# A chain of attention and two expert layers on one core: another order for the product of two weight matrices, three staging slots, and a last contraction made in halves

## The chip, the core and the metric

The kernel runs on one core of a Trainium2 chip. The metric is device microseconds (us) of one execution, from its begin to its end. Five engines of the core are spoken of: PE (TensorE, the matmuls), DVE (VectorE), ACT (ScalarE), POOL (GpSimd) and SP (SyncE, which here only issues transfers). Each works through its own instructions strictly in order. Results of matmuls stand in eight PSUM banks, `bk0` to `bk7`; a bank can be written again when what it holds has been read. TensorE's clock has two levels, 1.2 and 2.4 GHz; the profile gives the mean that was granted in a stretch, as a share of the higher one.

## The reference, cut to what matters

```python
def _attn_ref(q, k, v):                      # batch 4, heads 8, seq 576, head_dim 64
    scores = (1.0 / np.sqrt(D)) * np.matmul(q, k.transpose(0, 1, 3, 2))
    mask_plain = (rel >= 0) & (rel < 32)                       # heads 0 to 3
    mask_dil = (rel >= 0) & (rel < 128) & (rel % 4 == 0)       # heads 4 to 7
    attn = softmax(np.where(mask, scores, -1e9))
    return np.matmul(attn, v)

def _moe_ref(x, w1, w2, w3, w_out):          # d_model 512, d_ff 1024
    h = (x @ w1) * (x @ w2) @ w3
    return h @ w_out

def _moe2_ref(x, w_gate, w_val, w_out):      # d_model 512, d_ff 1536
    g = x @ w_gate
    return (g / (1.0 + np.exp(-g)) * (x @ w_val)) @ w_out

def reference(...):
    x = attention output as (4 * 576, 8 * 64)                  # 2304 tokens x 512
    return _moe2_ref(_moe_ref(x, ...), ...)
```

The weights arrive as float64; q, k and v are float32.

## The kernel before

**Precision.** Each operand of a large matmul is held as a high and a low part (`to_parts`: ACT copies the high part, L163, and DVE subtracts it from the source for the low one, L164). One product is then three matmuls, high by high, high by low and low by high (`mm3`, L221 to L223). The float64 weights are turned into float32 by `to_float32`, one ACT instruction (L204) and two on DVE (L205, L206), and split (ACT L199, DVE L200).

**Stage 0, from the start to about 94 us: attention of the first batch and W = w3 @ w_out.** Since nothing stands between `w3` and `w_out`, their product W (1024 x 512) is made once. It is eight tiles of 128 rows, each a sum over eight blocks j of three matmuls 128x512, 192 matmuls. The weights come in blocks of 1 MB, two names each, in the order of the list `W_ORDER`, through five buffers (`raw0` to `raw2` and two parts of `early`) that are loaded again as soon as they are converted. A program of sixteen steps s (L469) gives the order: in the first eight the tiles 0 to 3 are summed on `bk4`, `bk5`, `bk0` and `bk1` (names `w3a`), in the last eight the tiles 4 to 7 on `bk2`, `bk3`, `bk0` and `bk1` (names `w3b`). Between the steps stand units of attention, of head pairs 0 to 3 of the first batch: for each pair two halves of scores (L326; DVE scale and mask L340, maximum L343, ACT exp L345, DVE L348 to L350), three transposes (L363, ACT copy `pt` L365) and two halves of values (L378), whose results `to_parts` writes into `x0`, the input of the first expert layer. The units take their PSUM banks from `att_banks` in turn, which is `bk6`, `bk7` and, until the fourth block has been converted, also `bk2` and `bk3` (L314, L468).

**Stage 1, about 87 to 430 us: the first expert layer by chunks of tokens.** Chunks 0 to 3 have 512 tokens, chunk 4 has 256. For each of eight k: `gate_a` (12 matmuls, then ACT L240 copies the bank to `ta`), `gate_b` (12 matmuls, then DVE L246 multiplies, and `to_parts` makes `p`) and the contraction with W of the k before (12 matmuls). Attention of the following batch is interleaved in chunks 0 to 2. The weights of the second layer are staged beside it (`quarters`): a block is converted, DVE makes four sums of quarters (L535 to L538), and seven operands are split, the high part by ACT (L517) and the low one by POOL (L518), into a stage tile of 896 KB, which SP stores to `wd` or `wod` in DRAM (L554). A block gives two stage tiles. There are two stage tiles that take turns; a copy L517 into one waits until the store of what it held has landed. In chunks 3 and 4 the two lie in `mid_u` (L600).

**Stage 2, about 425 us to the end: the second expert layer.** Three parts of 768 tokens, six steps each, by seven products instead of eight: for each step the products of `w_gate` and `w_val` (L704, 128x384), whose results are put together by ACT and DVE (L710 to L724) into `u`, and for every two steps a contraction with the third matrix (`units`, L749): its seven operands are made by `make` (DVE sums L627 and `to_parts`) into four slots `po0` to `po3`, and its matmuls (L782) go into `bk0` to `bk3`, from where DVE adds them to `acc` (L768). The contraction of q, the q-th such pair of nine, runs between the products of the pair after it. The last, q = 8, has none after it and runs alone at the end, before the result is stored (L771).

The order in which each engine takes its instructions is fixed ahead of the run by a scheduler, within what program order, tiles and banks allow. PE's order is the same in both kernels from the middle of chunk 0 to chunk 4.

## Time and profile before

| | us |
|---|---|
| three runs | 856.11, 857.17, 857.97 |
| median | 857.17 |
| the profiled execution | 856.14 |
| its span, first to last instruction | 854.4 |
| outside the span | 1.74 |

| engine | busy us | share of the span |
|---|---|---|
| PE | 827.0 | 97% |
| DVE | 527.4 | 62% |
| ACT | 427.0 | 50% |
| POOL | 131.6 | 15% |

The mean granted clock was 0.992. PE is busy in 97% of the span, so a reader looks for the stretches where it is not. Where the profile names a releaser of an idle stretch, it is the work whose end came last among those that the instruction waited for. Because matmuls are pipelined, the distance between the starts of two of them is what one costs in a row, and it is less than the duration shown.

### The profile page before, as it was taken

The numbers are of one execution on the slowest core, as the hardware profiler recorded it, in microseconds if no ns is written. First come the engines' busy times: TensorE is split into PE (matmuls) and PEld (weight loads), VectorE is DVE, ScalarE is ACT, GpSimd is POOL, SyncE is SP. The second block draws the span as 40 slices with busy tenths as digits, with TensorE's granted clock in tenths as the row PEclk, the third lists the DMA queues.
The fourth block names the chain that finished last, engine by engine and source line by source line (L and its number), as shares of the span: only waits on it lengthen the run. The fifth ranks groups of instructions, "written<-read, shape, count | busy, mean of one in ns | idle before, by whom it ended". The sixth has DMA issues, their size and how long they took to land.

```text
span 854.4 us, 13410 instructions
## 1 busy us (share of the span) xinstructions
PE 827.0 (97%) x4954; PEld 751.8 (88%) x4954; DVE 527.4 (62%) x890; ACT 427.0 (50%) x1002; POOL 131.6 (15%) x180
## 2 busy tenths in 40 slices
PE   7879999999999899999899999999999999999996
PEld 5668888888888788877799999999999999999996
DVE  5899966275526652444566646588645677554747
ACT  4697765465635554334455544354444454353422
POOL 1000144135502541064520000000000000000000
PEclk8999999999999999999999999999999999999999
DMA  9997557568655845666999877788978787977725
GB/s 283 342 318 258 173 159 251 160 194 300 174 176 180 263 149 163 203 208 202 317 323 362 312 249 256 244 297 274 323 260 259 238 269 239 319 260 250 243 77 169
DMA packets 93248, 207.09 MB, mean 242 GB/s; under 512 B 7424, under 2 KB 56704, under 8 KB 88448
## 3 DMA queue, kind: packets, MB, share of 16 engines
q1 hardware_dynamic: 90304, 201.53, 72.2%
q10 hardware_dynamic: 2880, 4.72, 1.6%
q8 instruction: 39, 0.64, 0.3%
q14 instruction: 25, 0.20, 0.1%
HBM read 162.45 MB, written 43.78 MB: 241 GB/s over the span
## 4 chain that ended last, share of the span: by engine, by line
PE 76%; DMA 12%; DVE 6%; ACT 3%; POOL 2%; issue 1%; SPq 1%; ACTq 0%; DVEq 0%; POOLq 0%
PE bk L221 23%; PE bk L222 23%; PE bk L223 23%; DMA raw<-w_in 4%; DMA early<-w_in 3%; PE bk L326 3%; POOL u L518 2%; DMA wd<-u 2%; PE bk L378 2%; DMA wod<-u 2%; PE bk L363 1%; DMA k<-k_in 1%; DVE raw L206 1%; DVE w L200 1%; ACT s L345 1%
## 5 line engine op out<-in xcount | busy, mean ns | idle before, releaser
L221 PE MATMUL bk<-x,w 128*128 128x512 f32 (+2 forms) x400 | 146.6, 367 | 3.9 <-ACT ta L240 3.9
L223 PE MATMUL bk<-x,w 128*128 128x512 f32 (+2 forms) x400 | 146.4, 366 | 0.0
L222 PE MATMUL bk<-x,w 128*128 128x512 f32 (+2 forms) x400 | 146.0, 365 | 0.1
L221 PE MATMUL bk<-w 128*128 128x384 f32 (+1 forms) x264 | 93.2, 359 | 0.2 <-ACT w L199 0.2
L222 PE MATMUL bk<-w 128*128 128x384 f32 (+1 forms) x264 | 92.5, 352 | 0.5 <-DVE w L200 0.5
L221 PEld LDWEIGHTS bk<-x,w 128*128 128x128 f32 x400 | 75.4, 188 | 16.1 <-ACT ta L240 6.7
L223 PE MATMUL bk<-w 128*128 128x384 f32 (+1 forms) x264 | 89.4, 350 | 0.0
L222 PE MATMUL bk<-po,wo 128*128 128x384 f32 x252 | 84.4, 336 | 1.4 <-DVE po L164 1.4
L221 PE MATMUL bk<-po,wo 128*128 128x384 f32 x252 | 83.5, 336 | 1.7 <-ACT po L163 1.7
L223 PE MATMUL bk<-po,wo 128*128 128x384 f32 x252 | 84.6, 336 | 0.0
L768 DVE TENSOR_TENSOR acc<-bk,acc 128x384 f32<-128x384 f32 x102 | 55.8, 553 | 46.2 <-PE bk L223 46.0
L222 PEld LDWEIGHTS bk<-x,w 128*128 128x128 f32 x400 | 75.4, 189 | 10.1 <-DVE x L164 0.5
L223 PEld LDWEIGHTS bk<-x,w 128*128 128x128 f32 x400 | 75.4, 189 | 9.6
L518 POOL TENSOR_TENSOR stage<-raw,stage 128x256 fp32r<-128x256 f32 x88 | 63.9, 754 | 59.0 <-ACT stage L517 59.0
L163 ACT ACTIVATE po<-u 128x768 fp32r<-128x768 f32 x63 | 52.5, 843 | 31.3 <-PE bk L223 15.3
L710 ACT ACTIVATE u<-bk 128x384 f32<-128x384 f32 x80 | 38.8, 490 | 56.7 <-PE bk L223 55.6
L164 DVE TENSOR_TENSOR po<-u,po 128x768 fp32r<-128x768 f32 x63 | 59.6, 952 | 8.9 <-ACT po L163 8.8
L204 ACT ACTIVATE raw<-raw 128x1024 f32<-128x1024 f32 (+1 forms) x33 | 37.4, 1133 | 49.7 <-DMA raw<-w_in 49.7
L246 DVE TENSOR_TENSOR ta<-bk,ta 128x512 f32<-128x512 f32 (+1 forms) x40 | 25.4, 634 | 57.3 <-PE bk L223 28.4
L222 PE MATMUL bk<-p,W 128*128 128x512 f32 (+1 forms) x160 | 58.9, 373 | 0.2 <-DVE p L164 0.2
L223 PE MATMUL bk<-p,W 128*128 128x512 f32 (+1 forms) x160 | 58.9, 372 | 0.0
L221 PE MATMUL bk<-p,W 128*128 128x512 f32 (+1 forms) x160 | 57.1, 376 | 1.8 <-ACT p L163 1.8
(114 smaller groups left out, 1748.7 us busy)
## 6 DMA issues: line engine op xcount, KB each, us to landing
w<-wd SPq DMA_DIRECT2D x70, 512.0 KB, 4.6
wo<-wod SPq DMA_DIRECT2D x63, 512.0 KB, 4.7
raw<-w_in SPq DMA_DIRECT2D x31, 1024.0 KB, 9.0
mid<-wd SPq DMA_DIRECT2D x42, 512.0 KB, 4.6
wd<-stage SPq DMA_DIRECT2D x16, 896.0 KB, 6.3
wd<-u SPq DMA_DIRECT2D x8, 896.0 KB, 5.0
x<-wd SPq DMA_DIRECT2D x14, 512.0 KB, 4.5
v<-v_in SPq DMA_DIRECT2D x16, 432.0 KB, 8.2
```

The lines of the kernel that those rows point to most:

```text
L163: nc.scalar.activation(hi, src, AF.Copy)
L164: return nc.vector.tensor_tensor(out=lo, in0=src, in1=hi.bitcast(F32), op=ALU.subtract)
L204: nc.scalar.activation(hi.bitcast(F32), hi.bitcast(F32), AF.Prelu, scale=REBIAS, alpha=SIGN_UP)
L221: nc.tensor.matmul(ps, wh, xh, start=start, stop=False, skip_group_check=onto)
L222: nc.tensor.matmul(ps, wh, xl, start=False, stop=False, skip_group_check=onto)
L223: nc.tensor.matmul(ps, wl, xh, start=False, stop=stop, skip_group_check=onto)
L246: nc.vector.tensor_tensor(out=u, in0=bb[:, :n], in1=ta[:, :n], op=ALU.mult)
L326: nc.tensor.matmul(ps[:, (n - b0) * KW:(n - b0 + 1) * KW], q[:, QB + 2 * QB * n:QB + 2 * QB * (n + 1)], kk[:, n * QB:n * QB + KW], start=T ...
L378: nc.tensor.matmul(ps[j * D:(j + 1) * D, lo - a:hi - a], v_of(i)[:KW, n, j * D:(j + 1) * D], pt[:KW, n, (j + n) % 2 * QB + lo - n * QB:(j ...
L518: nc.gpsimd.tensor_tensor(out=dst[:, :, 1], in0=src, in1=dst[:, :, 0].bitcast(F32), op=ALU.subtract)
L710: nc.scalar.activation(t, src, AF.Copy)
L768: nc.vector.tensor_tensor(out=a, in0=ps, in1=a, op=ALU.add)
```

## The change

It has three parts.

*The product W and attention before chunk 0.* The same twelve blocks of weights, each as large as before, come in another order, and the columns of `w3` are cut into three pieces: `w3a` (tiles 0 to 3, as before), `w3c` (tiles 4 and 5) and `w3d` (tiles 6 and 7). The tiles 4 and 5 are summed on `bk2` and `bk3` while tiles 0 to 3 are summed on their four banks; then tile 6 is made over all j on `bk2`, and tile 7 on `bk3`. `att_banks` is `bk6` and `bk7` from the start. The matmuls that the blocks converted so far allow are 12, 24, 24, 48, 48, 72, 72, 96, 120, 144, 168, 192 before, and 12, 24, 36, 48, 72, 72, 96, 108, 120, 144, 168, 192 after.

*Staging in chunks 3 and 4.* There are three stage tiles instead of two, in `mid_u` from column block 1 on, and the low parts are subtracted by DVE instead of POOL: 56 instructions, 42 of 128x256 and 14 of 128x128. In chunks 0 to 2 two stage tiles and POOL remain.

*The last contraction.* The operands of q = 8 are made in two halves of 128x384, one for each step j of its pair: the first halves during the last products (`half(0)`), the second ones after (`half(1)`). Two of every six operands go to slots in `w_all` (`spare_ops`), the others to `po0` to `po3`.

```diff
-for _j in range(2, K1, 2):
-    W_ORDER += [(("wo1", _j), ("wo1", _j + 1)), (("w3a", _j), ("w3a", _j + 1))]
-W_ORDER += [(("w3b", j), ("w3b", j + 1)) for j in range(0, K1, 2)]
+for _name, _j in ("w3c", 0), ("wo1", 2), ("w3a", 2), ("wo1", 4), ("w3a", 4), ("w3c", 2), ("wo1", 6), ("w3a", 6), ("w3d", 0), ("w3d", 2):
+    W_ORDER.append(((_name, _j), (_name, _j + 1)))
...
+W_NEEDS = [1, 2, 3, 4, 5, 5, 7, 7, 8, 9, 10, 10, 11, 11, 12, 12]
...
-            att_banks = batt + acc[2:]
+            att_banks = batt
...
-            for upto in (2, 9, 16):
-                next_block()
-                attend(upto)
             next_block()
-            del att_banks[2:]
-            for s in range(2 * K1):
...
+            attend(2)
+            def w_step(name, i):
+                w3 = slot_of[name, i]
+                if name == "w3a":
+                    js, tiles, banks = [i], range(4), [ba, bb, acc[0], acc[1]]
+                elif name == "w3c":
+                    js, tiles, banks = [2 * i, 2 * i + 1], range(4, 6), acc[2:]
+                else:
+                    js, tiles, banks = range(i % 2 * 4, i % 2 * 4 + 4), [6 + i // 2], [acc[2 + i // 2]]
...
+            for s, step in enumerate(W_STEPS):
+                while n_split[0] < min(W_NEEDS[s] + 1, N_W1) and free:
                     next_block()
...
+                w_step(*step)
+                attend(min(4 * s + 5, done_at[1]))
...
             def split_to(dst, src):
                 nc.scalar.activation(dst[:, :, 0], src, AF.Copy)
-                nc.gpsimd.tensor_tensor(out=dst[:, :, 1], in0=src, in1=dst[:, :, 0].bitcast(F32), op=ALU.subtract)
+                (nc.gpsimd if len(stages) == 2 else nc.vector).tensor_tensor(out=dst[:, :, 1], in0=src, in1=dst[:, :, 0].bitcast(F32), op=ALU.subtract)
...
-                    stage = stages[n_stage[0] % 2]
+                    stage = stages[n_stage[0] % len(stages)]
...
-            stages[:] = [mid_u.rearrange("p n t -> p (n t)")[:, 8 * HT + i * 1792:8 * HT + (i + 1) * 1792].bitcast(F32R) for i in range(2)]
+            stages[:] = [mid_u.rearrange("p n t -> p (n t)")[:, HT + i * 1792:HT + (i + 1) * 1792].bitcast(F32R) for i in range(3)]
...
+            def made_at(q, r):
+                if q == NQ - 1:
+                    return spare_ops[r % 6] if r % 6 < 2 else late[0][(NPROD * q + r - 2) % NPO]
+                return late[0][(NPROD * q + r) % NPO]
...
+            def half(j):
+                if not halves[j]:
+                    u = uq[(NQ - 1) % 2]
+                    halves[j] = list(enumerate(sums([[u[:, 0, j], u[:, 1, j]], [u[:, 2, j], u[:, 3, j]]], C_ORDER)))[::-1]
+                r, of = halves[j].pop()
+                o = made_at(NQ - 1, r)
+                to_parts(of(), o[:, 0, j], o[:, 1, j])
...
                             if m == 1:
                                 load_wo(t + NWO)
+                                if q == NQ - 2 and 3 <= r < 6 or q == NQ - 1 and r == 0:
+                                    half(0)
+                                if q == NQ - 1 and r < NPROD - AHEAD1:
+                                    half(1)
...
+                        if n == FP * NC2 - 1:
+                            if m == 0 and i < 2:
+                                half(0)
+                            if m and i in (S3, S4):
+                                half(1)
```

What stands on three engines at three places follows. Lines of the changed kernel lie further down by 4 at the first place (L164, L200, L205, L206, L398 and L340 become L168, L204, L209, L210, L402 and L344), by 4 and 12 at the second (L163 and L240 become L167 and L244, L517 becomes L529), and by up to 29 at the third (L627, L722 and L768 become L639, L734 and L797). `raw0`, `raw1`, `raw2` and `early` are buffers of arriving weights, `w` is the memory of converted ones, `W2` and `W3` are tiles 4 to 7 of W, and `bk` is a bank.

DVE, at the end of stage 0, up to the last piece of `x0` (head pair 3), before:

```order
L206 SCALAR_TENSOR_TENSOR raw2_108<-raw2_108 128x1024
L200 TENSOR_TENSOR w_66<-raw1_79,w_66 128x2x512
L164 TENSOR_TENSOR W2_74<-bk2_84,W2_74 128x512
L164 TENSOR_TENSOR W2_74<-bk3_85,W2_74 128x512
L205 TENSOR_SCALAR raw0_78<-raw0_78 128x1024
L200 TENSOR_TENSOR w_66<-raw2_108,w_66 128x2x512
L164 TENSOR_TENSOR W3_75<-bk0_82,W3_75 128x512
L206 SCALAR_TENSOR_TENSOR raw0_78<-raw0_78 128x1024
L164 TENSOR_TENSOR W3_75<-bk1_83,W3_75 128x512
L164 TENSOR_TENSOR x0_76<-bk6_88,x0_76 128x2x128
```

The same place after:

```order
L168 TENSOR_TENSOR W3_75<-bk3_85,W3_75 128x512
L210 SCALAR_TENSOR_TENSOR raw2_108<-raw2_108 128x1024
L204 TENSOR_TENSOR w_66<-raw1_79,w_66 128x2x512
L209 TENSOR_SCALAR raw0_78<-raw0_78 128x1024
L204 TENSOR_TENSOR w_66<-raw2_108,w_66 128x2x512
L210 SCALAR_TENSOR_TENSOR raw0_78<-raw0_78 128x1024
L168 TENSOR_TENSOR x0_76<-bk7_89,x0_76 128x2x128
L402 COPY o0_80<-bk7_89 128x2x16
L168 TENSOR_TENSOR x0_76<-bk6_88,x0_76 128x2x128
```

The tiles of W have moved ahead of the conversions; the conversions themselves, of the same blocks of w1 and w2, still stand ahead of the last piece of `x0`.

ACT, in chunk 3, at the second staged block (`raw0`; `u` is the stage tile, `ta` the first gate, `p` the operand of the contraction), before:

```order
L240 ACTIVATE ta_68<-bk4_86 128x512
L517 ACTIVATE u_2876<-raw1_79 128x2x128 x4
L163 ACTIVATE p_77<-ta_68 128x512
L517 ACTIVATE u_2876<-raw0_78 128x2x128
L517 ACTIVATE u_2876<-raw0_78 128x128
L240 ACTIVATE ta_68<-bk4_86 128x512
L517 ACTIVATE u_2876<-raw0_78 128x2x128 x5
```

The same place after:

```order
L244 ACTIVATE ta_68<-bk4_86 128x512
L529 ACTIVATE u_2876<-raw1_79 128x2x128 x4
L167 ACTIVATE p_77<-ta_68 128x512
L244 ACTIVATE ta_68<-bk4_86 128x512
L529 ACTIVATE u_2876<-raw0_78 128x2x128
L529 ACTIVATE u_2876<-raw0_78 128x128
```

The copy to `ta` has moved ahead of the first copies of the second block into a stage tile.

DVE, after the last product's results (`g`), in the last contraction (`po` and, after, `w` are its operands), before:

```order
L768 TENSOR_TENSOR acc_3803<-bk0_82,acc_3803 128x384
L722 TENSOR_TENSOR u_2876<-bk5_87,g_2874 128x384
L627 TENSOR_TENSOR u_2876<-u_2876 128x768
L164 TENSOR_TENSOR po1_3796<-u_2876,po1_3796 128x768
L768 TENSOR_TENSOR acc_3803<-bk2_84,acc_3803 128x384
L164 TENSOR_TENSOR po3_3798<-u_2876,po3_3798 128x768
L627 TENSOR_TENSOR u_2876<-u_2876 128x768
L164 TENSOR_TENSOR po0_3795<-u_2876,po0_3795 128x768
```

The same place after:

```order
L168 TENSOR_TENSOR po1_3796<-u_2876,po1_3796 128x384
L734 TENSOR_TENSOR u_2876<-bk5_87,g_2874 128x384
L168 TENSOR_TENSOR po2_3797<-u_2876,po2_3797 128x384
L797 TENSOR_TENSOR acc_3803<-bk2_84,acc_3803 128x384
L797 TENSOR_TENSOR acc_3803<-bk1_83,acc_3803 128x384
L168 TENSOR_TENSOR w_66<-u_2876,w_66 128x384
L797 TENSOR_TENSOR acc_3803<-bk3_85,acc_3803 128x384
L168 TENSOR_TENSOR po0_3795<-u_2876,po0_3795 128x384
```

Behind the last multiplication (L722, now L734) operands of 128x768 with their sums have given way to halves of 128x384; their first halves stand ahead of it.

## Rows read from the trace of the kernel before

**Rows 1.** Windows: length; PE, PEld, DVE, ACT, POOL busy (count); clock; DMA; GB/s

```profile
9.28:53.46 44.18, 35.81 (x233) 28.98 (x233) 36.59 (x67) 31.61 (x90) 0.00 (x0) 0.89 1.05 338
40.33:93.82 53.49, 49.04 (x322) 39.76 (x320) 51.74 (x78) 42.72 (x83) 0.00 (x0) 0.97 0.84 283
50.00:60.00 10.00, 7.13 (x30) 6.05 (x31) 10.00 (x17) 8.91 (x20) 0.00 (x0) 0.83 0.98 274
365.00:430.00 65.00, 59.03 (x300) 49.04 (x299) 32.83 (x51) 26.98 (x64) 33.19 (x45) 1.00 0.77 252
829.60:836.48 6.88, 5.44 (x32) 5.12 (x31) 6.88 (x12) 2.89 (x4) 0.00 (x0) 1.00 0.35 88
```

**Rows 2.** Timeline of PE, stage 0: start, duration, line, operation [idle before <-releaser]

```profile
53.46 2.02 PE L326 MATMUL bk<-k,q 128*128 128x96 f32 x8
...
86.70 0.39 PE L223 MATMUL bk<-w 128*128 128x512 f32 x1
86.93 0.39 PE L221 MATMUL bk<-x,w 128*128 128x512 f32 x1
...
93.87 0.50 PE L222 MATMUL bk<-x,w 128*128 128x512 f32 x1
```

**Rows 3.** Timeline of DVE, stage 0

```profile
40.33 0.70 DVE L205 TENSOR_SCALAR raw<-raw 128x1024 uint32<-128x1024 uint32 x1 [2.78 <-DMA raw<-w_in]
40.94 1.12 DVE L340 SCALAR_TENSOR_TENSOR s<-bk,mask 128x480 f32<-128x480 f32 x2
...
93.21 0.60 DVE L164 TENSOR_TENSOR x<-bk,x 128x256 fp32r<-128x256 f32 x1
```

**Rows 4.** Waits of PE by releaser, 365 to 430 us: total us, times, longest

```profile
PE bk L221 <- ACT ta L240: 3.9, 5, 1.1
...
PE bk L221 <- ACT p L163: 1.8, 1, 1.8
```

**Rows 5.** Timeline of all engines, chunks 3 and 4

```profile
363.89 4.90 POOL L518 TENSOR_TENSOR u<-raw,u 128x256 fp32r<-128x256 f32 x6
...
365.71 1.31 DVE L164 TENSOR_TENSOR p<-ta,p 128x512 fp32r<-128x512 f32 x1 [1.14 <-ACT p L163]
...
369.91 0.43 DVE L535 TENSOR_TENSOR raw<-raw 128x256 f32<-128x256 f32 x1
...
374.22 0.63 ACT L517 ACTIVATE u<-raw 128x256 fp32r<-128x256 f32 x2 [8.54 <-DMA wod<-u]
...
375.39 0.50 PE L221 MATMUL bk<-x,w 128*128 128x512 f32 x1 [0.80 <-ACT ta L240]
...
377.86 0.69 DVE L164 TENSOR_TENSOR p<-ta,p 128x512 fp32r<-128x512 f32 x1 [1.80 <-ACT p L163]
...
426.38 1.17 ACT L204 ACTIVATE raw<-raw 128x1024 f32<-128x1024 f32 x1 [1.76 <-DMA raw<-w_in]
```

**Rows 6.** Transfers issued in 365 to 430 us: KB each, median us to landing

```profile
wd<-u SPq DMA_DIRECT2D x8, 896.0 KB, 5.0
raw<-w_in SPq DMA_DIRECT2D x5, 1024.0 KB, 9.2
wod<-u SPq DMA_DIRECT2D x4, 896.0 KB, 6.8
```

**Rows 7.** Timeline of PE at the end

```profile
832.97 0.33 PE L221 MATMUL bk<-w 128*128 128x384 f32 x1
...
833.49 0.33 PE L221 MATMUL bk<-po,wo 128*128 128x384 f32 x1
...
836.48 0.44 PE L222 MATMUL bk<-po,wo 128*128 128x384 f32 x1 [1.44 <-DVE po L164]
...
840.17 0.79 PE L221 MATMUL bk<-po,wo 128*128 128x384 f32 x3 [1.67 <-ACT po L163]
...
850.70 0.34 PE L223 MATMUL bk<-po,wo 128*128 128x384 f32 x1
```

**Rows 8.** Timeline of DVE at the end

```profile
835.47 0.95 DVE L164 TENSOR_TENSOR po<-u,po 128x768 fp32r<-128x768 f32 x1
```

More of the change, by code (lines that the diff above doesn't have):

```diff
@@ L83 @@
 NPO = 4
+AHEAD1 = 4
 NWO = 4
@@ L104, in moe_chain_kernel @@
         fp = first_pool.__enter__()
-        wslot = [w_all[:, i] for i in (6, 1, 3, 0, 5, 2, 7, 4)] + [fp.tile([P, 2, 2, 512], F32R, name=f"W{i}") for i in range(4)]
+        wslot = [w_all[:, i] for i in (2, 3, 7, 4, 0, 6, 1, 5)] + [fp.tile([P, 2, 2, 512], F32R, name=f"W{i}") for i in range(4)]
         xb = [fp.tile([P, 2, KT, CMAX], F32R, name="x0")]
@@ L463, in moe_chain_kernel @@
             free.extend(wslot[:8])
-            for upto in (2, 9, 16):
-                next_block()
-                attend(upto)
             next_block()
-            del att_banks[2:]
-            for s in range(2 * K1):
-                h, j = divmod(s, K1)
-                while n_split[0] < min(s // 2 * 2 + 4, N_W1) and free:
-                    next_block()
-                wo, w3 = slot_of["wo1", j], slot_of["w3b" if h else "w3a", j]
-                banks = [acc[2], acc[3], acc[0], acc[1]] if h else [ba, bb, acc[0], acc[1]]
-                for kk in range(4):
-                    c = slice(kk * P, (kk + 1) * P)
-                    mm3(banks[kk], (w3[:, 0, c], w3[:, 1, c]), (wo[:, 0], wo[:, 1]), j == 0, j == K1 - 1)
-                if j == K1 - 1:
-                    for kk in (2, 3, 0, 1):
-                        w = wslot[8 + 2 * h + kk // 2][:, kk % 2]
-                        slot_of["W", 4 * h + kk] = w
-                        to_parts(banks[kk], w[:, 0], w[:, 1])
-                release(("w3b" if h else "w3a", j))
-                if h:
-                    release(("wo1", j))
-                attend(min(4 * s + 4, done_at[1]))
+            attend(2)
@@ new lines, in w_step @@
+            def w_step(name, i):
[6 more added lines that the diff above has]
+                    js, tiles, banks = range(i % 2 * 4, i % 2 * 4 + 4), [6 + i // 2], [acc[2 + i // 2]]
+                n = 0
+                for j in js:
+                    wo = slot_of["wo1", j]
+                    for ps in banks:
+                        c = slice(n * P, (n + 1) * P)
+                        mm3(ps, (w3[:, 0, c], w3[:, 1, c]), (wo[:, 0], wo[:, 1]), j == 0, j == K1 - 1)
+                        n += 1
+                if js[-1] == K1 - 1:
+                    for kk, ps in zip(tiles, banks):
+                        w = wslot[8 + kk // 2][:, kk % 2]
+                        slot_of["W", kk] = w
+                        to_parts(ps, w[:, 0], w[:, 1])
+                release((name, i))
+                if name == "w3d" and i >= 2:
+                    release(*[("wo1", j) for j in js])
@@ L747, in load_wo @@
                     nc.sync.dma_start(out=dst.bitcast(F32), in_=src.bitcast(F32))
+            def made_at(q, r):
+                if q == NQ - 1:
+                    return spare_ops[r % 6] if r % 6 < 2 else late[0][(NPROD * q + r - 2) % NPO]
+                return late[0][(NPROD * q + r) % NPO]
+            NQ = FP // 2 * NC2
+            spare_ops = [ops[i] for i in range(NOP) if (i - NPROD * (NC2 - 1)) % NOP >= NPROD]
+            halves = [[], []]
+            def half(j):
[5 more added lines that the diff above has]
+                to_parts(of(), o[:, 0, j], o[:, 1, j])
             def units(q):
                 u = uq[q % 2]
-                made = deque(enumerate(sums([[u[:, 0], u[:, 1]], [u[:, 2], u[:, 3]]], C_ORDER)))
+                made = deque(enumerate(sums([[u[:, 0], u[:, 1]], [u[:, 2], u[:, 3]]], C_ORDER)) if q < NQ - 1 else [])
                 c, first = divmod(q, FP // 2)
@@ L758, in make @@
                         r, of = made.popleft()
-                        o = late[0][(NPROD * q + r) % NPO]
+                        o = made_at(q, r)
                         to_parts(of(), o[:, 0], o[:, 1])
@@ L778, in unit @@
                             t = NPROD * q + r
-                            w, x = late[1][t % NWO], late[0][t % NPO]
+                            w, x = late[1][t % NWO], made_at(q, r)
                             ps = cbank[m][s in (S1, S4, A12)][:, :HT]
@@ L816, in moe_chain_kernel @@
                             step()
+                        if n == FP * NC2 - 1:
[3 more added lines that the diff above has]
+                                half(1)
                 if n % 2:
                     units(n // 2)
+            half(0)
+            for _ in range(AHEAD1 - 2):
+                half(1)
             contract_some(99)
@@ L864, in layouts @@
         "w3a": lambda j: rows(w3t, j)[:, :512],
-        "w3b": lambda j: rows(w3t, j)[:, 512:],
+        "w3c": lambda j: np.concatenate([rows(w3t, 2 * j + i)[:, 4 * P:6 * P] for i in range(2)], 1),
+        "w3d": lambda j: np.concatenate([rows(w3t, j % 2 * 4 + i)[:, (6 + j // 2) * P:(7 + j // 2) * P] for i in range(4)], 1),
         "w1": lambda j: cols(w1, j),
```

2 lines of the change are left out of this document (added).

## The prediction, made before the change was run

> **What bounds the kernel now.** PE is busy in 97% of the span, so I looked for the stretches in which it is not, first in the windows, then in each stretch with the waits and the timelines. Three stretches matter, and each has another limit.
>
> *Stage 0.* In 9.28 to 53.46 us PE is busy for 35.81 of 44.18 us [rows 1], 8.4 us idle, at a granted clock of 0.89. From 53 us on it runs through: the last matmul of the product W starts at 86.70, the first of chunk 0 at 86.93 [rows 2]. But DVE tells more. From 40.33 us, where it has waited 2.78 us for weights, to 93.82 us, when the last piece of `x0` is done (L164 at 93.21, 0.60 long) [rows 3], it is busy for 51.74 of 53.49 us [rows 1]. PE needs that piece for its matmul at 93.87 [rows 2]. So DVE, not the product, sets when chunk 0 can go on. PE's idle time before was not lost; it only let PE come out at the time at which DVE was ready.
>
> *Staging in chunks 3 and 4.* In 365 to 430 us PE is busy for 59.03 of 65.00 us [rows 1], 5.97 idle: 3.9 waiting for ACT's copy to `ta` in five stalls, 1.8 for its copy to `p` in one [rows 4], and short rests. ACT is busy for only 26.98 us there. The chain is seen at 374.22: the first copy L517 into a stage tile has waited 8.54 us for the store `wod<-u` of what the tile held; the copy to `ta` stands behind it, and PE goes on at 375.39, 0.80 late [rows 5].
>
> *The end.* The last product's matmuls end ahead of 833.49. Then PE runs the last contraction and stops at 836.48 for 1.44 us (DVE's `po`) and at 840.17 for 1.67 us (ACT's `po`); its last matmul starts at 850.70 [rows 7]. DVE has no pause in 829.60 to 836.48 [rows 1].
>
> **Part 1, the product W.** The 192 matmuls, the twelve blocks, their bytes and their conversions remain. What PE can start earlier it starts earlier: 36 matmuls instead of 24 after the third block. The 8.4 us of idle time could so go, and the product end at about 78.5 instead of 86.9. What comes next is the last piece of `x0`. From the L205 that waits at 40.33 up to that piece DVE has the same instructions in both orders, conversions of the blocks 6 to 17 and half of block 18, eight pieces of W, six of `x0`, four softmax halves, but for two that have moved ahead of 40.33 and so into the 2.78 us of waiting: a mask (half of 1.12 for two [rows 3]) and a maximum of the same size, 1.1 us together. If DVE has no pauses, the piece is done at 40.33 + 51.7 - 1.1 = 91.0; with all its pauses of before, at 93.8 - 1.1 = 92.7. I take the middle, 91.9: 2.0 us gained. Against it stands the clock. PE will now stand idle for much of the ten microseconds between the end of the product and this piece, as it did in 50 to 60 us, where the granted clock was 0.83 with PE busy for 7.13 of 10 us [rows 1]. A mean of 0.83 is a third of the time at 1.2 GHz; it costs up to 0.17 x 10 = 1.7 us if the matmuls behind it run in it, nothing if none does; I take 1.1, nearer to the full price, since matmuls follow at once. Net 0.9 us gained. Bounds: 2.8 gained (no pause, no clock lost) and 1.5 lost (the pauses of before leave 1.2 of gain, the full clock price takes 1.7, and 1.0, another pause of DVE like those that it has now in sum, if two banks instead of four hold up a softmax).
>
> The Trainium skill (Perfetto Trace Analysis, Identifying Performance Opportunities) says that the same gap coming again and again on the engine that should be saturated can mean too few SBUF or PSUM buffers for the next tile. That speaks against taking two of attention's four banks away; if the trace followed it, the loss would be that of the rival on pair 3 below. The trace of before can't settle it: it shows the scores on four banks, and none that waits long for one.
>
> **Part 2, staging.** 5.97 us of idle time, and each of the six stalls is followed by a matmul 0.50 instead of 0.39 long [rows 2, 5], 0.7 in all: 6.7 us to be had. A block gives two tiles at once. With two slots, the first tile of a block waits for the first of the block before, whose store takes 5.0 to 6.8 us to land at the median [rows 6]; with three, each tile has at least one block more time, and a k of 36 matmuls at 0.227 (86.70 to 86.93 [rows 2]) is 8.2 us long. In chunk 3 this takes the wait away: ACT's copy to `ta` has also moved ahead of the second block's copies. In chunk 4 a k is about half as long, a block needs 9.2 us to land [rows 6], ACT waited 1.76 us for one at 426.38 [rows 5], and a third slot does nothing for that. I keep 2.0 us of stalls there, between 0 and 4. So 4.7 gained, from 2.7 to 6.7.
>
> The subtraction moves from POOL (4.90 for six [rows 5], 0.82 each) to DVE, where 128x256 takes 0.43 [rows 5]: 56 x 0.43 = 24 us at the most. DVE is busy for 32.83 of 65 us there [rows 1], 57 at the most after. Some of that comes back: L164 took 1.31 us at 365.71, within POOL's 4.90 from 363.89, and 0.69 at 377.86 [rows 5], and POOL now rests. What it adds is a wait: DVE's subtraction now stands in order behind ACT's copy, and if that copy waits for a slot, DVE's L246 and L164 wait behind it. They need ACT's `ta` and `p` anyway, which stand behind the same copy, so I cost it at nothing; without that cover each wait would be worth a stall like those of before, about 1 us, and the lower end above holds two of them.
>
> **Part 3, the end.** Behind the last product 78 matmuls remain before, 72 after (six move ahead of it). From 832.97 to 833.49 are three steps, 0.173 each [rows 7], so without a stall the last would start at 833.49 + 77 x 0.173 = 846.8 rather than at 850.70: 3.9 us of stalls, 3.1 in the two large ones. The six that move change nothing in the sum. Afterwards the first halves of the operands are made before the last product ends, and what follows DVE's last multiplication is a half each, instead of operands of 128x768 at 0.95 us [rows 8] with their sums. Halving costs more per element (0.43 for 256 columns against 0.69 for 512 [rows 5]), some 14 extra instructions in all, which DVE has room for after 836.48, not before. I see no operand that comes late by more than a few tenths, and keep 0.6 us for reads of banks. So 3.3 gained; at worst 1.5 (one of the two stalls stays), at best 3.9. The store after it, 3.4 us from the last matmul to the end, stays.
>
> **Sum.** 0.9 + 4.7 + 3.3 = 8.9 us off the profiled 856.14: 847.2. That execution lies 1.03 below the median of 857.17, so 848.3 for the median. The ends of the terms give 13.4 (843.8) and 2.7 (854.5).
>
> **The rivals.**
> *DVE is not the limit of stage 0.* If earlier tiles of W let DVE skip ahead and the piece of `x0` comes as early as the product, all 8.4 us come back: 848.3 - 7.5 = 840.8. Against it: 51.7 us of DVE work that is still there.
> *Transfers limit the staging, and stage 0 gives nothing.* The DMA share is 0.77 in 365 to 430 us and 0.84 in stage 0 [rows 1]; a faster ACT asks for blocks earlier and waits for their 9.2 us. Then staging gives half, 2.5, stage 0 nothing: 857.17 - 2.5 - 3.0 = 851.7.
> *Nothing is gained, for the change doesn't do what it says.* The stalls of staging turn into waits for blocks, PE's clock eats what stage 0 brings, and the end still waits for one operand: 857 or a little under.
> *Slower: attention on two banks delays pair 3.* The second half of its scores runs on PE at 53.46 now [rows 2]; 40.4 us later PE has its `x0`. With two banks each unit waits until ACT or DVE has read the one before the last. I estimate the scores at 60 from the units ahead of them, which is still ahead of DVE's queue. If they come after 63, the chain of softmax, transposes and values, if it remained as long as now, would bring the piece after 103; that is 9.5 us more than 93.9, less than the rest gains by 1.5. At 65 the piece would come at 105, 11 us late: 857.2 + 11 - 8.0 = 860.
>
> **How the numbers follow.** The forecast has 0.62, the early `x0` 0.06, the transfers 0.17, no gain 0.08, slower 0.07. About two in ten lie outside 843.8 to 854.5, to which the forecast and the transfers belong with nearly all of theirs. This kernel can be told from no change by about 0.2%, 1.7 us: faster 0.85, same 0.08, slower 0.07.
>
> **What would show it.** In the profile after: the last piece of `x0` between 91 and 92.7 us, PE idle before it for several us, at a lower clock; no L221 wait for `ta` over 0.3 us in chunk 3, some in chunk 4; no POOL row in chunks 3 and 4; the last matmul within 13.5 us of the last product. Wrong would be: a piece of `x0` much earlier or later, waits of DVE for ACT's copies into stage tiles with PE behind, or a stall of over 1 us in the last contraction.

## The result, and the profile after

The changed kernel takes 847.77 us at the median (six runs, 845.88 to 852.09), the kernel before, run beside it, 859.31. Their ratio, taken over all these runs, is 0.9883, 95% interval 0.9848 to 0.9918 (the two medians alone would give 0.9866). Its profiled execution took 847.58 us, span 845.6; the forecast for that sum was 847.2, and 848.3 for the median. In two later jobs the ratio was 0.9901 (0.9871 to 0.9931) and 0.9917 (0.9886 to 0.9947).

Page of the changed kernel, part 1, and its windows, of which the third, fourth and sixth answer to [rows 1]. Columns as there. Lines of the changed kernel lie 4 to 29 further down, as said with the change.

```profile
PE 825.4 (98%) x4954; PEld 751.7 (89%) x4954; DVE 539.6 (64%) x957; ACT 429.4 (51%) x1009; POOL 89.2 (11%) x124
...
9.28:53.46 44.18, 39.25 (x236) 32.19 (x237) 37.85 (x62) 31.99 (x82) 0.00 (x0) 0.92 1.05 335
40.33:93.82 53.49, 47.85 (x322) 38.47 (x321) 52.43 (x79) 45.58 (x86) 0.00 (x0) 0.95 0.86 289
...
80.00:90.00 10.00, 5.48 (x61) 4.06 (x60) 10.00 (x14) 6.84 (x10) 0.00 (x0) 0.95 0.50 158
90.00:95.00 5.00, 4.89 (x16) 3.87 (x17) 4.82 (x10) 2.84 (x3) 0.00 (x0) 0.50 0.40 154
95.00:100.00 5.00, 5.00 (x31) 4.44 (x30) 4.53 (x11) 3.94 (x15) 0.00 (x0) 0.92 0.44 117
365.00:430.00 65.00, 63.28 (x348) 54.99 (x347) 47.48 (x109) 31.60 (x75) 0.00 (x0) 1.00 0.87 287
```

The kernel before, the same windows at the end of stage 0:

```profile
80.00:90.00 10.00, 10.00 (x79) 7.98 (x78) 9.69 (x14) 9.17 (x13) 0.00 (x0) 1.00 0.61 211
90.00:95.00 5.00, 4.88 (x28) 3.89 (x26) 5.00 (x9) 1.97 (x4) 0.00 (x0) 1.00 0.44 177
```

PE is idle for 1.7 of the 65 us from 365 to 430, where it had been idle for 5.97. In 80 to 90 it is idle for 4.5 us, where it had run through, and the clock granted right behind is 0.50, the lower of its two levels, where it had been 1.00.

To see where the time went, the start of the same matmul was read in the traces of before and of the other kernel at five places: the first of the contraction with W in chunk 1, in chunk 3 at k = 2 (the 313th of these matmuls), the first of the second layer's contraction, the first of its last pair (q = 8), and the very last. The differences between neighbouring places, in us (minus is earlier than before):

| kernel | to chunk 1 | chunks 1, 2 | chunks 3, 4 | stage 2 | end | sum |
|---|---|---|---|---|---|---|
| changed, first | +0.16 | -0.38 | -5.24 | 0.00 | -3.27 | -8.73 |
| changed, again | -0.22 | +1.05 | -5.18 | 0.00 | -3.28 | -7.63 |
| changed, third | -0.72 | +4.88 | -2.97 | 0.00 | -3.27 | -2.08 |
| a_old_product | -0.64 | +1.75 | -4.44 | 0.00 | -3.30 | -6.63 |
| product_only | -0.19 | +2.86 | -1.45 | 0.00 | -0.16 | +1.06 |
| b_three_pool | -0.42 | +0.62 | +0.03 | 0.00 | -3.27 | -3.04 |
| c_two_dve | -0.47 | -0.87 | +3.84 | -1.04 | -3.26 | -1.80 |
| d_old_tail | -0.46 | +2.57 | -5.10 | 0.00 | -0.11 | -3.10 |
| e_warm | -4.65 | +13.33 | -2.54 | 0.00 | -3.30 | +2.84 |
| f_pool_w | +2.77 | +1.64 | -4.67 | 0.00 | -3.28 | -3.54 |
| g_warm8 | +0.76 | +4.97 | -5.64 | 0.00 | -3.26 | -3.17 |
| h16 | -4.74 | +9.46 | -2.53 | 0.00 | -3.27 | -1.08 |
| h15 | -6.91 | +6.19 | -4.68 | 0.00 | -3.27 | -8.67 |

The first row is the answer for that execution: nothing from the product W, 5.2 from staging, 3.3 from the end. How far one execution can be trusted is told by the columns in which kernels are alike. In chunks 1 and 2, where PE's order is the same in both kernels, three executions of the changed kernel differ by 5 us. Windows from the mark of chunk 1 to that of chunk 3, of the first and of the third:

```profile
188.90:371.49 182.59, 180.61 (x1128) 148.84 (x1126) 94.49 (x186) 93.71 (x283) 56.81 (x77) 1.00 0.62 200
188.02:375.87 187.85, 184.38 (x1127) 151.06 (x1126) 95.09 (x185) 94.38 (x284) 57.79 (x77) 0.98 0.60 194
```

The third has 1.5 us more of idle time, and a mean clock of 0.98 over 188 us is worth 3 to 4 us: that is nearly all of the difference. In chunks 3 and 4 the three executions have -5.24, -5.18 and -2.97, and product_only, with the staging of before, has -1.45. Before has one trace only, so a size read there is sure only to about 2 us. The other rows are the experiments, below.

Stage 0 of the changed kernel, PE's timeline and then DVE's (start, duration, line, operation, idle before and releaser), to be read beside [rows 2, 3]:

```profile
77.91 0.39 PE L227 MATMUL bk<-w 128*128 128x512 f32 x1
78.14 0.39 PE L225 MATMUL bk<-x,w 128*128 128x512 f32 x1
...
82.95 0.53 PE L367 MATMUL bk<-ident,s 128*96 128x128 f32 x3 [1.46 <-DVE o L402]
...
89.75 1.22 PE L225 MATMUL bk<-x,w 128*128 128x512 f32 x2 [2.13 <-ACT x L167]
91.08 2.45 PE L330 MATMUL bk<-k,q 128*128 128x96 f32 x10
93.23 0.77 PE L226 MATMUL bk<-x,w 128*128 128x512 f32 x1
93.81 0.63 PE L227 MATMUL bk<-x,w 128*128 128x512 f32 x1
```

```profile
39.97 0.69 DVE L209 TENSOR_SCALAR raw<-raw 128x1024 uint32<-128x1024 uint32 x1 [1.97 <-DMA raw<-w_in]
...
88.01 1.21 DVE L204 TENSOR_TENSOR w<-raw,w 128x1024 fp32r<-128x1024 f32 x1
89.15 1.22 DVE L210 SCALAR_TENSOR_TENSOR raw<-raw 128x1024 uint32<-128x1024 uint32 x1
...
90.90 0.61 DVE L168 TENSOR_TENSOR x<-bk,x 128x256 fp32r<-128x256 f32 x1
```

The last matmul of the product starts at 77.91 instead of 86.70, DVE goes on with conversions, and the last piece of `x0` starts at 90.90 instead of 93.21. From DVE's wait for weights at 39.97 to the end of this piece there are 51.55 us; before, from the wait at 40.33, there were 53.48 [rows 3]. In the other two executions of the changed kernel and in product_only the wait ends at 39.18, 38.24 and 38.84, and the piece is done 51.55, 51.57 and 51.54 us later. So DVE sets the time of the piece, the new order is worth 1.9 us of it, and the rest is weights that landed earlier. That is not the order's doing: in a_old_product, with the old order, the wait ended at 38.87, and the piece was done 54.33 us later.

But the matmul that needed the piece starts at 93.23, only 0.64 earlier than the 93.87 of before, since ten score matmuls ahead of it now run at the lower clock (2.45 us; before, at 89.93, 1.25), and the matmuls behind it are 0.63 long instead of 0.39.

Chunk 4, ACT; then chunk 4 and the end, PE:

```profile
420.07 1.16 ACT L208 ACTIVATE raw<-raw 128x1024 f32<-128x1024 f32 x1 [1.81 <-DMA raw<-w_in]
421.14 0.36 ACT L244 ACTIVATE ta<-bk 128x256 f32<-128x256 f32 x1
```

```profile
421.55 0.39 PE L225 MATMUL bk<-x,w 128*128 128x256 f32 x1 [1.57 <-ACT ta L244]
...
828.89 0.33 PE L227 MATMUL bk<-w 128*128 128x384 f32 x1
...
835.77 0.45 PE L225 MATMUL bk<-po,wo 128*128 128x384 f32 x1 [0.30 <-DVE acc L797]
...
841.97 0.34 PE L227 MATMUL bk<-w,wo 128*128 128x384 f32 x1
```

PE's first row is its only listed wait in 365 to 430 us (before: [rows 4, 5]): ACT had waited 1.81 us for a block to land, with the copy to `ta` behind. From the last product to the last matmul there are 13.1 us with one wait of 0.30, against 17.4 with 1.44 and 1.67 in [rows 7].

### The profile page after: what moved, and what is told of

It reads as the page before. It is cut to its first block, busy times and chain, and to the rows that moved or that the text cites. A ratio compares the mean times of both kernels' runs of the same rounds, so it can differ in the third digit from the quotient of the medians.

```text
span 845.6 us, 13394 instructions
## 1 busy us (share of the span) xinstructions
PE 825.4 (98%) x4954; PEld 751.7 (89%) x4954; DVE 539.6 (64%) x957; ACT 429.4 (51%) x1009; POOL 89.2 (11%) x124
## 4 chain that ended last, share of the span: by engine, by line
PE 75%; DMA 9%; DVE 9%; ACT 4%; issue 2%; SPq 0%; ACTq 0%; DVEq 0%
PE bk L225 23%; PE bk L226 23%; PE bk L227 23%; DMA raw<-w_in 6%; PE bk L330 2%; ACT s L349 2%; DVE raw L210 2%; PE bk L382 2%; DVE w L204 1%; PE bk L367 1%; DVE raw L209 1%; DVE u L530 1%; DMA q<-q_in 1%; DMA raw<-x1d 1%; DVE early L210 1%
## 5 line engine op out<-in xcount | busy, mean ns | idle before, releaser
L797 DVE TENSOR_TENSOR acc<-bk,acc 128x384 f32<-128x384 f32 x102 | 55.8, 553 | 44.7 <-PE bk L227 44.5
L227 PE MATMUL bk<-po,wo 128*128 128x384 f32 x240 | 80.6, 336 | 0.0
L226 PE MATMUL bk<-po,wo 128*128 128x384 f32 x240 | 80.3, 335 | 0.0
L225 PE MATMUL bk<-po,wo 128*128 128x384 f32 x240 | 79.5, 336 | 0.3 <-DVE acc L797 0.3
L722 ACT ACTIVATE u<-bk 128x384 f32<-128x384 f32 x80 | 38.6, 489 | 53.6 <-PE bk L227 53.6
L167 ACT ACTIVATE po<-u 128x768 fp32r<-128x768 f32 (+1 forms) x64 | 50.9, 803 | 26.2 <-PE bk L227 10.5
L168 DVE TENSOR_TENSOR po<-u,po 128x768 fp32r<-128x768 f32 (+1 forms) x64 | 57.4, 901 | 8.7 <-ACT po L167 8.6
L349 ACT ACTIVATE s<-s,sm 128x96 f32<-128x96 f32 x144 | 52.0, 364 | 11.4 <-DVE sm L347 11.0
```

The costliest lines, as they stand in the source:

```text
L167: nc.scalar.activation(hi, src, AF.Copy)
L168: return nc.vector.tensor_tensor(out=lo, in0=src, in1=hi.bitcast(F32), op=ALU.subtract)
L225: nc.tensor.matmul(ps, wh, xh, start=start, stop=False, skip_group_check=onto)
L226: nc.tensor.matmul(ps, wh, xl, start=False, stop=False, skip_group_check=onto)
L227: nc.tensor.matmul(ps, wl, xh, start=False, stop=stop, skip_group_check=onto)
L349: nc.scalar.activation(s[:, n], s[:, n], AF.Exp, bias=m[:, 0, n:n + 1], accum_out=m[:, 1, n:n + 1])
```

## The experiments

The kernels a, b, c and d each take back one thing. All differences below are against the changed kernel unless another is named; where a sum over the run is within the spread of chunks 1 and 2, the stage's own column of the table is read, and the whole time is given beside it.

**The product's part undone (a_old_product), and alone (product_only).** The first has the order of blocks, the steps and the banks of before, with the changed staging and end; the second is the kernel before with only the new order of blocks, steps and banks.

```diff
-            att_banks = batt
+            att_banks = batt + acc[2:]
...
```

> The changed kernel with the product of w3 and w_out, the order of the weight blocks and attention's four banks put back as before; staging and last contraction stay changed. Theory 1, from the two traces: the product's part brings nothing, because what it gains before the last piece of x0 (90.90 instead of 93.21 us) is paid back by TensorE's clock, which was granted at 0.50 in 90 to 95 us. Then this kernel takes as long as the changed one within 1 us (about 8.5 us less than before), its last piece of x0 comes at about 93 us and its clock is 1.00 in 90 to 100. Theory 2: the low clock is an accident of one execution and the product's part is worth its 2.3 us: then this kernel is 2 to 2.5 us slower than the changed one.

Measured: ratio to before 0.9936 (0.9909 to 0.9964), the last piece of `x0` at 92.57, near the 93.21 of before, and the clock at 1.00 behind it (windows):

```profile
80.00:90.00 10.00, 10.00 (x81) 8.04 (x80) 9.69 (x13) 9.18 (x13) 0.00 (x0) 1.00 0.58 198
90.00:95.00 5.00, 5.00 (x29) 4.07 (x29) 4.52 (x9) 2.09 (x2) 0.00 (x0) 1.00 0.35 139
```

PE is busy for all ten microseconds there. At chunk 1 this kernel stands at -0.64, the changed one at +0.16, -0.22 and -0.72: up to there nothing is gained by the new order, as theory 1 has it. The whole time does not bear theory 1 out. By the ratios a is 1.6 to 4.5 us slower than the changed kernel of the three jobs (0.9917 to 0.9883), more than theory 1's 1 us, and theory 2's 2 to 2.5 lie within.

> The kernel before with the first part of the change alone (order of the weight blocks, W over six banks, attention on two). Theory 1: nothing is gained, within 1 us of before: the last piece of x0 ends between 90.5 and 92 us, 2 us earlier, and the clock of 0.5 in 90 to 95 takes it back. Theory 2: the 2 us are real: 2 to 2.5 us faster than before.

Measured: ratio 0.9986 (0.9954 to 1.0018), clock 0.50 in 90 to 95, last piece of `x0` at 89.78 for 0.60 us (ends at 90.4, a little earlier than expected), -0.19 at chunk 1. Up to chunk 1 both kernels agree with theory 1: the 2 to 4 us by which the piece comes earlier do not reach it. For the whole time product_only is 1.2 us faster than before, with an interval from 3.9 faster to 1.5 slower. So whether the product's part gives up to some 3 us behind chunk 1 is open; in chunks 1 and 2 single executions differ by more than that.

**Three slots with POOL (b_three_pool), two slots with DVE (c_two_dve).**

```diff
-                (nc.gpsimd if len(stages) == 2 else nc.vector).tensor_tensor(out=dst[:, :, 1], ...
+                nc.gpsimd.tensor_tensor(out=dst[:, :, 1], ...
```

```diff
-            stages[:] = [mid_u...[:, HT + i * 1792:HT + (i + 1) * 1792].bitcast(F32R) for i in range(3)]
+            stages[:] = [mid_u...[:, HT + i * 1792:HT + (i + 1) * 1792].bitcast(F32R) for i in range(2)]
+            c_pool[0] = False
...
-                (nc.gpsimd if len(stages) == 2 else nc.vector).tensor_tensor(out=dst[:, :, 1], in0=src, ...
+                (nc.gpsimd if c_pool[0] else nc.vector).tensor_tensor(out=dst[:, :, 1], in0=src, ...
```

(`c_pool` keeps POOL in chunks 0 to 2 and DVE in chunks 3 and 4, which the number of tiles told apart before.)

> The changed kernel with POOL making the low parts in chunks 3 and 4, three stage tiles kept. Theory 1: the slots were the limit (ACT waited for a store to land), so three slots with POOL keep at least 4 of the 5.2 us that staging gained: PE idle in 365 to 430 us under 3 us, the kernel at most 1.5 us slower than the changed one. Theory 2: POOL's 0.82 us for each of seven subtractions holds the store back, and that is what filled the slots: PE idle there over 4 us, the kernel 3 to 5 us slower than the changed one. The copy to ta stands behind a block's first copies into the stage tile again in this kernel's ACT order.

> The changed kernel with two stage tiles instead of three, the low parts on DVE. Theory 1 (slots are the limit): ACT's copies wait for stores to land again, PE is idle for 4 us or more in 365 to 430, and the kernel is 3 to 5 us slower than the changed one. Theory 2 (POOL's time is): the tiles are stored some 3 us earlier, two slots do, PE idle stays under 3 us, and the kernel is at most 1.5 us slower than the changed one.

Measured: ratios 0.9963 (0.9938 to 0.9988) and 0.9991 (0.9966 to 1.0015); in chunks 3 and 4 +0.03 and +3.84 us against before, where the changed kernel has -5.24, -5.18 and -2.97. By the ratios b is 4 to 7 us slower than the changed kernel of the three jobs and c 6 to 9. Neither half of the staging part gives its gain by itself. Theory 1 fails for b, and theory 2 for c; b has theory 2's number, but not by its mechanism, and c loses more than theory 1's 3 to 5.

With three slots and POOL the wait for stores is nearly gone. ACT's waits for them in 345 to 440 us (total, times, longest), two rows of before and then b's:

```profile
ACT u L517 <- DMA wod<-u: 15.0, 3, 8.5
ACT u L517 <- DMA wd<-u: 13.8, 5, 4.1
...
ACT u L529 <- DMA wod<-u: 3.2, 1, 3.2
```

But another wait stands in its place. POOL, PE and ACT in b, chunk 4, three timelines, and a window:

```profile
407.39 6.14 POOL L530 TENSOR_TENSOR u<-raw,u 128x256 fp32r<-128x256 f32 x8 [5.67 <-ACT u L529]
```

```profile
426.60 0.38 PE L225 MATMUL bk<-x,w 128*128 128x256 f32 x1 [2.89 <-ACT ta L244]
```

```profile
425.13 1.15 ACT L208 ACTIVATE raw<-raw 128x1024 f32<-128x1024 f32 x1 [3.29 <-DMA raw<-w_in]
426.18 0.36 ACT L244 ACTIVATE ta<-bk 128x256 f32<-128x256 f32 x1
```

```profile
425.00:430.00 5.00, 3.40 (x17) 3.40 (x18) 4.39 (x7) 2.56 (x5) 1.34 (x2) 0.71 1.02 327
```

POOL reads the block until 413.5; a block's buffer is loaded again when its last reader has done, and the next block is landed at 425.1. ACT waits 3.29 us for it, with the copy to `ta` behind, PE stands for 2.89, and a clock of 0.71 in these five microseconds costs 1.5 more. In c the older wait is back, ACT's waits in 345 to 440 us (total, times, longest) and PE's timeline:

```profile
ACT u L531 <- DMA wd<-u: 14.4, 6, 4.0
```

```profile
411.26 0.50 PE L225 MATMUL bk<-p,W 128*128 128x512 f32 x1 [2.03 <-ACT p L167]
```

So there are two queues in a row, the stage tiles and the blocks' buffers. A third tile opens the first, DVE's shorter subtraction empties the second, and ACT stands behind whichever is the longer. That the load is late because POOL held the buffer follows from the rows' times and the program; it was not tried with another buffer. That c is slower even than before was not taken apart; its longest waits there are PE's for `p`, 4.8 us in three from the mark of chunk 3 to the second layer's contraction, against 1.8 in one.

**The end undone (d_old_tail).** The last contraction makes its operands whole, as before.

```diff
-                        o = made_at(q, r)
+                        o = late[0][(NPROD * q + r) % NPO]
```

> The changed kernel with the last contraction's operands made whole, as before. Theory 1: the halves are worth 3.3 us by themselves: PE stops again for DVE's and ACT's po behind the last product, 3.1 us in two stalls, and the kernel is 3.3 us slower than the changed one (2.5 to 4). Theory 2: part of the 3.3 comes from how the parts before shift the last steps: under 2 us.

Measured: ratio 0.9954 (0.9928 to 0.9980), 3 to 6 us slower than the changed kernel of the three jobs. The end column is -0.11 instead of -3.27, and -0.16 in product_only, which has the old end too; in the eleven executions with halves it lies between -3.26 and -3.30. PE's waits in 820 to 855 us (total, times, longest) are the two of [rows 7] again:

```profile
PE bk L224 <- ACT po L166: 1.7, 1, 1.7
PE bk L225 <- DVE po L167: 1.4, 1, 1.4
```

**PE kept at work in the idle time (e_warm, g_warm8).** Matmuls whose result nobody reads, into `bk0`.

```diff
+            def keep_warm(g, n):
+                t = pt[:KW, 3 * g:3 * g + 3]...bitcast(BF16)...
+                for _ in range(n):
+                    nc.tensor.matmul(acc[0][:, :3 * P], t[:, :P], t, start=True, stop=True)
+            keep_warm(0, 6)
+            keep_warm(2, 14)
```

> The changed kernel with 20 matmuls of 128x384 without use for the output put on PE into its idle time of 85 to 90 us: six behind the last transposes of pair 3, fourteen behind its values, into a bank that is free there. Theory 1 (the clock takes back what the product's part gains): the granted clock in 90 to 95 us is 0.9 or more and the kernel is 2 to 2.9 us faster than the changed one. Theory 2 (the clock is a mark of waiting and costs little): the time is that of the changed one within 0.5 us, or up to 1 us longer, for the extra matmuls.

Windows of e_warm:

```profile
80.00:90.00 10.00, 8.76 (x85) 6.21 (x86) 10.00 (x17) 6.70 (x9) 0.00 (x0) 1.00 0.63 215
90.00:95.00 5.00, 4.89 (x27) 4.08 (x26) 4.70 (x9) 3.48 (x6) 0.00 (x0) 1.00 0.47 108
```

The clock stays at 1.00, and at chunk 1 the kernel stands at -4.65, 3.9 to 4.8 us ahead of the three executions of the changed one. That is more than the clock's price, 2.9 us by the first execution's 0.50 in 90 to 95 and 0.92 in 95 to 100. About half a microsecond of it is six transposes that stand behind this mark here; and the last piece of `x0` started at 88.73 in this execution, 2.2 earlier than in the first, but only by 0.5 earlier than the 89.21 of the third. Then it loses 13.3 us in chunks 1 and 2, and the whole is 10 us slower than the changed kernel in the same job (ratio 1.0019, 0.9986 to 1.0051), which neither theory had. The added instructions changed the scheduler's order there (attention's units stand up to some 40 large matmuls later than in the changed kernel). The window between the two marks:

```profile
184.09:380.39 196.30, 186.48 (x1134) 151.51 (x1133) 100.78 (x192) 94.74 (x289) 65.43 (x80) 0.98 0.58 186
```

PE is idle for 9.8 us there, 7.8 more than in the changed kernel's first execution, most of it in attention's units, which wait for DVE and ACT, and the clock of 0.98 is worth 3 to 4 us. That the new order is the cause of these waits was not tried by itself. So another form, which leaves the orders alone, eight matmuls of 128x512 from `x0` ahead of the second transposes:

```diff
+                    if c == k == 0:
+                        for _ in range(8):
+                            nc.tensor.matmul(acc[0], x[:, 1, 2, :P], x[:, 1, 2], start=True, stop=True)
```

> The changed kernel with eight matmuls of 128x512 without use for the output between the first and the second transposes of pair 3, and every engine's order else as in the changed kernel through stage 1 (in e_warm the orders of chunks 0 to 2 had changed with it). Theory 1 (the clock is what the product's part pays with): clock 0.9 or more in 90 to 95 us, and the kernel 2 to 3 us faster than the changed one, now to the end. Theory 2 (the matmuls only move the idle time): they hold up the transposes by 1.8 us, the last piece comes later by as much, and nothing is gained.

Windows of g_warm8:

```profile
80.00:90.00 10.00, 6.94 (x67) 5.10 (x65) 10.00 (x15) 6.90 (x11) 0.00 (x0) 0.99 0.50 163
90.00:95.00 5.00, 4.40 (x15) 3.95 (x16) 4.22 (x8) 2.67 (x3) 0.00 (x0) 0.50 0.31 116
```

Ratio 0.9927 (0.9903 to 0.9951), beside 0.9917 for the changed kernel in the same job. The piece comes at 90.58, so the matmuls did not hold it up; but the clock fell all the same, and nothing was gained. Theory 2 has that result, but not its reason, the late piece. It does not decide what a kept clock is worth to the end of the run; that stays with e_warm's first column.

**DVE relieved in stage 0 (f_pool_w, h16, h15).** First by giving POOL the subtractions of six weight blocks, then by converting the last blocks later.

```diff
-                nc.vector.tensor_tensor(out=w[:, :, 1], in0=x, ...
+                (nc.gpsimd if 13 <= n < N_W1 - 1 else nc.vector).tensor_tensor(out=w[:, :, 1], in0=x, ...
```

> The changed kernel with POOL instead of DVE making the low parts of the last weight blocks of w1 and w2 (L204, blocks 13 to 18), five of them ahead of the last piece of x0 in DVE's order. Theory 1 (DVE's work sets when x0 is complete): the last piece comes 5 x 1.14 = 5.7 us earlier, at about 85.5 us, PE's idle time before it falls below 2 us, the clock stays at 1.00, and the kernel is 4 to 7 us faster than the changed one. Theory 2 (POOL's reads hold up DVE's, or the weights' transfers are next): the piece comes at 88 or later and the kernel gains under 3 us, or loses.

Measured: ratio 0.9944 (0.9908 to 0.9979), 3 us slower than the changed kernel in the same job, +2.77 at chunk 1; the last piece of `x0` at 93.51, behind a wait of 2.99 us for ACT's copy. Timelines of DVE and of POOL:

```profile
75.69 2.19 DVE L209 TENSOR_SCALAR raw<-raw 128x1024 uint32<-128x1024 uint32 x1
77.80 2.81 DVE L354 TENSOR_TENSOR s<-s,sm 128x384 f32<-128x384 f32 x1
80.53 3.42 DVE L210 SCALAR_TENSOR_TENSOR raw<-raw 128x1024 uint32<-128x1024 uint32 x1
...
92.29 0.61 DVE L168 TENSOR_TENSOR x<-bk,x 128x256 fp32r<-128x256 f32 x1 [2.99 <-ACT x L167]
```

```profile
73.84 6.35 POOL L204 TENSOR_TENSOR w<-early,w 128x1024 fp32r<-128x1024 f32 x2 [69.92 <-ACT w L203]
80.15 2.71 POOL L204 TENSOR_TENSOR w<-raw,w 128x1024 fp32r<-128x1024 f32 x1
```

While POOL works, a DVE row of the kind L210 that takes 1.22 us above takes 3.42, and one of the kind L209 (L205 before, 0.70 in [rows 3]) takes 2.19. The Trainium skill (SBUF — State Buffer, Who interferes with whom) has a rule for it: a DVE instruction with two SBUF inputs contends with a POOL instruction that reads SBUF, and the lock on the ports that they share is exclusive. The two longer rows agree with it; the first has one SBUF input and is longer too, which this rule alone does not cover. So this experiment does not tell what less work on DVE is worth: from 40.33 us to the end of the piece DVE is busy for 50.0 us, in the changed kernel for 50.3.

```diff
                 while n_split[0] < N_W1 and free:
-                    next_block()
+                    (next_block_behind_p if n_split[0] >= 16 else next_block)()
```

> The changed kernel with the conversion of weight blocks 16 to 19 put behind the first p of chunk 0, which takes two and a half conversions (7.5 us of DVE) out of DVE's order ahead of the last piece of x0. Theory 1 (DVE's work sets when x0 is complete): the piece comes by 83 to 86 us instead of 90.9, PE idles under 2 us before it, the clock stays at 1.00 in 90 to 95, and PE's first contraction of chunk 0 starts 5 to 8 us earlier (at 96 to 99 us). Theory 2 (the chain scores, transposes, values is next): the piece comes at 87 or later. For the whole time: as much faster as chunks 0 to 2 keep, where the orders change too and e_warm lost 13 us; 3 to 8 us faster than the changed one if they keep it.

> As h16, with block 15 behind the first p as well (2.9 us of DVE more). Theory 1: the last piece of x0 no earlier than in h16 by more than 1 us, since the chain of pair 3 is then the limit; the whole time within 3 us of h16. Theory 2 (DVE is the limit even there): 2.9 us earlier again.

Windows of h15, and DVE's last piece of `x0`:

```profile
80.00:90.00 10.00, 8.83 (x91) 7.75 (x90) 5.96 (x15) 5.87 (x20) 0.00 (x0) 1.00 0.06 17
90.00:95.00 5.00, 5.00 (x28) 4.25 (x27) 5.00 (x9) 3.46 (x17) 1.27 (x1) 1.00 0.34 103
```

```profile
83.59 0.61 DVE L168 TENSOR_TENSOR x<-bk,x 128x256 fp32r<-128x256 f32 x1 [2.96 <-ACT x L167]
84.21 0.60 DVE L168 TENSOR_TENSOR x<-bk,x 128x256 fp32r<-128x256 f32 x1
```

With conversions out of the way the last piece comes at 84.21 (h15) and 87.02 (h16) instead of 89.2 to 90.9, the clock is 1.00, PE's first contraction starts at 95.41 and 97.43 instead of 103.2 to 104.1, and at chunk 1 the kernels stand at -6.91 and -4.74. For h16 the piece is theory 2's, the clock and PE's first contraction are theory 1's: of the 7.5 us taken off DVE only about 3 reach the piece, and DVE now waits for ACT's copy ahead of it, 2.96 us in h15's row above: the chain of pair 3 has become the limit. In h15 the piece comes 2.8 earlier again, not within the 1 us of theory 1; with DVE no longer working through, it is the chain that runs earlier there (ACT has the block's two copies less ahead of it, too), which was not tried apart. What is settled is that the conversions ahead of the piece held PE up: put later, they leave PE 4 to 7 us ahead of the changed kernel at chunk 1, clock and all. The whole time profits little. Chunks 1 and 2 take back 6.2 (h15) and 9.5 us (h16), and the ratios are 0.9907 (0.9871 to 0.9943) for h15 and 1.0002 (0.9975 to 1.0029) for h16, against 0.9917 for the changed kernel in the same job. For the whole time h15 is 8.7 us faster than h16, which theory 1 did not allow either. Their orders in chunks 1 and 2 differ from the changed kernel's, as in e_warm. Between the two marks PE is idle for 4.8 us in h15 and 7.6 in h16, against 2.0 in the changed kernel's first execution, at a clock of 0.99 and 0.98; which move in these orders makes the waits is open. None of the versions here beats the changed kernel by more than its interval.

## Why the prediction was right, point by point

*The sum* was 847.2 for the profiled execution, and 847.58 was measured. Of the three terms the end was right in size and reason, staging was right in size for half a reason, and stage 0 was too high by 0.2 to 1.1 us. That the sum came within 0.4 is in part luck: it has no term for chunks 1 and 2, which moved by 5 us between three executions, and the one that was profiled first had -0.38 there. The third, with the same kernel, had its last matmul only 2.1 us earlier than before.

*Stage 0, which part limits.* Predicted: the product ends at about 78.5, the last piece of `x0` is done between 91.0 and 92.7, PE idle before it. Measured: chunk 0 starts at 78.14, the piece is done at 91.5, and PE is idle for 4.5 us in 80 to 90. In the other two executions the piece is done at 90.7 and 89.8, earlier than the band, which took DVE's wait for weights to end at 40.33 as in the one trace of before; counted from where it did end, DVE saved 1.9 us in each of them, where 2.0 had been worked out. Counting DVE's instructions up to the piece, not PE's gaps, was the step that carried; h16 and h15 show it by moving the piece when conversions are taken out of the way.

*Stage 0, the clock.* The mis-sized term: 1.1 us, bounded by 1.7. The bound came from a mean of 0.83 over ten microseconds of before [rows 1]. Measured was 0.50 over 90 to 95 and 0.92 over 95 to 100, 2.5 and 0.4 us of work not done. With 2.3 gained at the piece this leaves about nothing, and +0.16, -0.22 and -0.72 were measured at chunk 1 where a gain of 0.9 had been forecast. A mean over a stretch that held only part of the slow time was no upper bound for another stretch. (In its lower bound 1.2 stands for the gain with the pauses of before; from 93.8 and 92.7 it is 1.1.)

*Staging.* Predicted 4.7 (2.7 to 6.7), measured 5.2, 5.2 and 3.0 in three executions; the remaining wait of 1.57 stands in chunk 4 behind a block that had not landed, as forecast, and chunk 3 has none. But the gain was put down to the third slot alone, with the move to DVE at no cost and no gain. b and c show that the slot alone brings nothing (+0.03) and DVE alone a loss (+3.84). The 0.7 us for slow first matmuls holds, though two of the six are 0.39 long and not 0.50, in chunk 4, where the others are 0.28.

*The end.* Predicted 3.3, measured 3.27. The working (the matmuls without a stall, 0.6 left for reads of banks) is confirmed by d, where the two stalls come back; what was left as a wait is one read of 0.30.

*The rivals.* Two banks for attention did put off pair 3's second half of scores, to 61.24 us from 53.46, near the 60 of the estimate, but the last piece came earlier all the same, since DVE's queue, and not the 40.4 us of before, lies between them; the longest wait of PE for a bank in stage 0 is the 1.46 us of the row at 82.95. (At 63 us that rival's loss of 9.5 us would exceed the 8.0 of the other two terms by 1.5; the sentence in the prediction reads the other way round.) That the whole 8.4 us would come back is what h15 nearly does in stage 0, by other means. Of the rival on transfers, stage 0 without a gain came true, but by the clock; ACT's waits for blocks did grow, from 8.3 to 14.2 us in 345 to 440, but staging gave more than its 2.5. A stall of one operand at the end, as in the rival without a gain, did not appear.

## What to carry to other kernels

Before an idle engine is given its work earlier, count what the next engine in the chain must still do until the point where both meet: here PE finished 8.8 us sooner and waited, and the wait cost it the clock. Where a chain has two buffers in a row, test both together, since neither opened alone showed a gain. When a stage's gain is smaller than the spread of a run, read it from the start of the same instruction in the two traces, and in more than one execution: the end's 3.3 us stood within 0.04 us in eleven executions whose last matmuls differ by 11.6, but the changed kernel's gain in chunks 3 and 4 moved by 2.3. And look at what else moved: between three executions of the same kernel the piece of `x0` came up to 1.7 us apart only because the weights landed at other times.

## What was not expected of the hardware

POOL beside DVE cost more than it relieved: subtractions of 2.4 to 3.2 us on POOL lengthened DVE's rows from 1.22 to 3.42 and from 0.70 to 2.19 us. And the clock stood at its lower level for all of 90 to 95 us, behind ten microseconds in which PE had been idle for 4.5.
